# Attention with routed experts on one core: scores read three times from PSUM, q in zero-padded whole-array tiles, x gathered from the output

## The chip, the cores and the metric

One NeuronCore of one Trainium2 chip runs the whole program. The metric is device microseconds of one execution. The profile names the engines: PE is TensorE (PEld its weight loads), DVE VectorE, ACT ScalarE, POOL GpSimd, SP the SyncE queue that issues most DMAs. TensorE's clock is granted at one of two levels, 1.2 and 2.4 GHz; the profile prints the granted clock as a share of 2.4 GHz.

## The reference

```python
scores = matmul(q, k.T) / sqrt(64)            # 8 batches x 8 heads, 576 x 576, head size 64
scores = where(scores >= max(scores) - tau, scores, -1e9)
attn = exp(scores - max(scores)); attn /= attn.sum(-1) + 1e-9
x = (attn @ v) as (4608 tokens, 512)          # heads side by side
do_compute = x @ w_skip > 0                   # others: out = x
e = argmax(x @ w_gate)                        # one of 8 experts, weight gw from a softmax
out = x + gw * (relu(x @ w1[e]) @ w2[e])      # 512 -> 1024 -> 512
```

All inputs and the output are float32.

## The kernel before

The work has two parts. The attention part goes through 32 pairs of heads (8 batches, 4 pairs each). Of a pair's 576 query rows it takes four chunks of 128 rows, each for both heads, and a fifth chunk of the two heads' 64 last rows, one head above the other. A chunk has a unit per head, the fifth chunk one unit for both, so a pair has nine units, each with 128 rows by 576 scores. The expert part then runs nine jobs: one job for the fullest expert, picked early, and one per expert.

A unit before the change goes this way. `score` (line 516) makes the scores in two PSUM banks: the two heads lie in rows 0 to 63 and 64 to 127 of the array, and their matmuls run beside each other (the last chunk: `score_m`, line 525). `top` (line 540) is one custom DVE instruction that reads the two banks, scales by -1/8, writes the result `s` to SBUF and takes its minimum, which is minus the row's largest score. The banks are free when it is done; there are two slots of two banks (`NSL`), and a chunk takes both. `thr` (line 556) makes the threshold on POOL or DVE, `expo` (line 561) the exponential on ACT from `s`, `mask` (line 571) keeps p where `s` is under the threshold, on DVE, with both inputs in SBUF (four buffers `s`, `SB`; three chunks of p, `PFB`). Then `fph` (line 606) rounds p to float16 on ACT or DVE, `fpl` (line 621) subtracts for the low half on POOL or DVE, `turn` (line 627) issues two DMA transposes on SP, and `plan_av` (line 642) multiplies by v with 30 matmuls. `plan_out` (line 680) divides by the row sums, `plan_logits` (line 786) makes the routing logits, `plan_rows` (line 830) and `plan_tails` (line 843) store x twice: to `out`, where it stays for skipped tokens, and to a second DRAM copy `xs`, from which the expert jobs gather. `plan_v` (line 369) splits a batch's v into float16 halves.

The order on every engine is fixed when the program is built: `Plan.run` (line 132) is a list scheduler with a cost per operation and offsets (`OFF`, line 74) to the due times; an operation allowed on several engines goes to the one that can start first. Rings (`ring.take`, `ring.free`) make an operation wait until the buffer's last user is done. Where PE would idle by the plan, `fill` (line 1374) issues matmuls on zeros whose result nobody reads. POOL, SP and the other queues run in order.

In the expert part `gather_x` (line 1411) gathers a job's rows with indirect DMAs on POOL, `prep_x` (line 1419) transposes them on PE, `store` (line 1480) writes results to `out` with indirect DMAs on POOL. For most jobs the next job's gather is queued right behind a job's stores.

Of the kernel before, what the change touches and what calls it, by code (L numbers as in the profile page):

```python
# [12 lines left out]
F32 = mybir.dt.float32  # L13
# [11 lines left out]
P = 128  # L25
S = 576
# [26 lines left out]
GPB = 2  # L53
SB = 4
PFB = 3
NSL = 2
TOP = 3.0e38
FILL = (0.4, 0.22, 0.6)
# [16 lines left out]
    ld=-63.5, qs=-113.0, S=-99.4, mx=-53.9, th=-2.3, e=-9.8, p=-0.5, ph=-18.0, pl=11.4, tt=-64.0, av=31.6, cp=-20.0, x=28.2, xw=39.6, row=38.9, rsp=74.8, init=19.6, L1=-102.6, sc=-126.0, d0=16.6, phD=43.5, v=45.4, vsp=-12.1, V2=35.8,  # L75
# [20 lines left out]
class Plan:  # L96
    def __init__(self):
        self.ops, self.rings, self.fill = [], {}, None
# [33 lines left out]
    def run(self, look):  # L132
# [14 lines left out]
        while left:  # L147
# [13 lines left out]
            if e == "PE":  # L161
                if self.fill and free[e] > 0:
                    gap = t - free[e] - FILL[0]
                    for _ in range(int(gap * FILL[2] / FILL[1]) if gap > 0 else 0):
                        self.fill(half)
                half = o.half
# [20 lines left out]
def attn_moe_kernel(ctx: ExitStack, tc: tile.TileContext, qk, vl, vt, tau, wg, w1, w2, out):  # L187
# [14 lines left out]
    xs = dp.tile([NTOK, DM], F32, name="xs")  # L202
    taub = cp.tile([P, 1], F32, name="taub")
    nc.scalar.dma_start(taub, tau.rearrange("(a b) -> a b", b=1).broadcast_to([P, 1]))
    tneg8 = cp.tile([P, 1], F32, name="tneg8")
    nc.vector.tensor_scalar(tneg8, taub, 0.0, -0.125, op0=ALU.is_ge, op1=ALU.mult)
    wgt = cp.tile([P, NDT, 16], F32, name="wgt")
    onesr = cp.tile([1, P], F32, name="onesr")
    none16 = cp.tile([P, S], BF16, name="none16")
    nc.vector.memset(none16, 0.0)  # L210
# [6 lines left out]
    nc.vector.tensor_scalar(taue, taub, 0.0, None, op0=ALU.max)  # L217
    lstc = lst.rearrange("(p c) b -> p c b", p=P)
# [9 lines left out]
    ps_s = att.enter_context(tc.tile_pool(name="ps_s", bufs=1, space=PSUM))  # L228
    sall = ps_s.tile([P, 2 * NSL, 512], F32, name="sps")
    slots = [(2 * i, 2 * i + 1) for i in range(NSL)]  # L230
    rest = ps_s.tile([P, 512], F32, name="rest")
# [7 lines left out]
    PTa = ep.tile([P, PTB, 2 * STEP, P], F16, name="PTa", tag="QK1")  # L239
    hls = [hla[:, i] for i in range(HLB)]  # L240
# [5 lines left out]
    TMs = [a1.tile([P, STEP + 1, P], F16, name=f"TM{i}") for i in range(2)]  # L246
    def settle_v():
        nc.vector.memset(vraw[TL:P, NTL : NTL + H, :], 0.0)
        nc.vector.memset(vraw[0:TL, NTL + H :, :], 0.0)
# [77 lines left out]
    def gather(dst, idx, n):  # L327
# [3 lines left out]
            xs[0:n, :],  # L331
# [14 lines left out]
    def init():  # L346
# [6 lines left out]
            xs[NTOK - S - TL : NTOK - S, :].rearrange("p (o c) -> p o c", c=P),  # L353
# [3 lines left out]
    def plan_pair(g):  # L357
        k = STEP * g

        def load():  # L360
            T["raw", g] = wtile(F32, "raw")[:, 0 : 2 * S]
            nc.sync.dma_start(T["raw", g], qk[g])

        o = pl.dma(k - OFF["ld"], load, ring.take("wr", WRB) + T["start"], [2.2], 0.46)
        T["in", g] = o
# [3 lines left out]
    def plan_v(b):  # L369
# [90 lines left out]
        for i, (t0, t1) in enumerate(((0, NTL // 2), (NTL, NBK), (NTL // 2, NTL))):  # L460
# [19 lines left out]
            off = {DVE: OFF["d0"]} if b else {}  # L480
            r = pl.op(kk, fr, [sc], {ACT: w / 1200 + 0.15, DVE: w / 1900 + 0.1}, off=off)
            c = pl.op(kk + 0.1, fh, [r], {ACT: w / 1200 + 0.15, DVE: w / 1900 + 0.1}, off=off)
            d = pl.op(kk + 0.2, fl, [c], {POOL: 0.00208 * w + 0.075, DVE: w / 960 + 0.1}, off=off)
# [10 lines left out]

    def plan_chunk(g, i):
# [4 lines left out]
        hs = (slice(0, D), slice(D, P))  # L500

        if M:
            pr = slots.pop(0)
            slots.append(pr)
            views = [sorted(pr)]
        else:
            p1, p2 = slots.pop(0), slots.pop(0)
            views = [sorted((p1[u], p2[u])) for u in units]
            order = [views[u].index(p1[u]) for u in units]
            slots.extend(tuple(v) for v in views)  # L510
# [1275 lines left out]
```

## Time and profile before

| | us |
|---|---|
| median of 3 runs | 1115.29 (1114.37 to 1116.28) |
| the profiled execution | 1115.98 |
| its span, first to last instruction | 1114.1 |
| busy: PE, DVE | 874.4, 892.6 |
| busy: ACT, POOL | 525.1, 637.0 |
| mean granted clock | 0.826 |

The attention part lasts until about 800 us, the expert part from there to the end. A share of busy time over the whole span mixes the two. In the rows, `L545` is line 545, `p<-s,mx,p` names what is written and read, `x288` counts instructions, and what follows `<-` behind an idle time is what ended it. A float32 matmul counts as two instructions.

### The profile page before, as it was taken

What the parts mean: (1) busy time and instruction counts of PE and PEld (TensorE: products, weight loads), DVE (VectorE), ACT (ScalarE), POOL (GpSimd) and SP (SyncE); (2) the same over time, 40 slices, a digit from 0 to 9 for tenths busy, and PEclk for the clock granted to TensorE, in tenths of its full rate; (3) what the DMA queues carried; (4) which work ended last, traced back from release to release, by engine and by line L of the source; (5) the groups of instructions that cost most, each with busy time, mean ns of one, the idle gap of its engine ahead of it and who ended that gap; (6) DMA issues with size and microseconds to landing.
All of it is one profiled execution on the core that took longest, in us unless ns stands there. A gap on an engine that the chain in (4) does not pass through costs nothing. (4 is left out here: it accounts for less than half of the span.)

```text
span 1114.1 us, 21828 instructions
## 1 busy us (share of the span) xinstructions
PE 874.4 (78%) x8443; PEld 659.3 (59%) x8443; DVE 892.6 (80%) x1587; ACT 525.1 (47%) x785; POOL 637.0 (57%) x441
## 2 busy tenths in 40 slices
PE   7767777678878667887767877677679899999995
PEld 4445545446655445555444645454467699899994
DVE  6999998988898899999998999988944354557871
ACT  2745545553544455454445655555423243344441
POOL 1866655765775667536754675577631454544561
PEclk8787789777786887887688689687968999999998
DMA  5696896798659779977867879567871644445530
GB/s 168 132 204 131 139 250 133 139 195 204 129 121 233 146 145 186 225 148 138 173 163 146 163 153 240 118 113 179 152 236 56 228 150 161 161 160 185 191 132 16
DMA packets 387784, 179.34 MB, mean 161 GB/s; under 512 B 354231, under 2 KB 354999, under 8 KB 387680
## 3 DMA queue, kind: packets, MB, share of 16 engines
q1 hardware_dynamic: 383056, 167.78, 66.6%
q0 software_dynamic: 4480, 10.15, 2.7%
q8 instruction: 67, 1.10, 0.4%
q14 instruction: 37, 0.30, 0.1%
q10 hardware_dynamic: 144, 0.00, 0.0%
HBM read 67.76 MB, written 24.65 MB: 83 GB/s over the span
## 5 line engine op out<-in xcount | busy, mean ns | idle before, releaser
L521 PE MATMUL sps<-raw 64*128 64x288 f32 x1024 | 227.0, 558 | 155.8 <-DVE mx L545 154.1
L623 POOL TENSOR_TENSOR hla<-p,hla 128x1152 f16<-128x1152 f32 x102 | 263.5, 2586 | 56.9 <-ACT hla L339 27.1
L574 DVE SCALAR_TENSOR_TENSOR p<-s,mx,p 128x576 f32<-128x576 f32 x256 | 280.5, 1120 | 4.5 <-POOL mx L559 2.3
L545 DVE CUSTOM_DVE_ANT_0 s<-sps,none,tneg 128x576 f32<-128x576 f32 x288 | 225.7, 810 | 54.6 <-PE sps L521 52.4
L567 ACT ACTIVATE p<-s,mx 128x576 f32<-128x576 f32 x256 | 187.7, 768 | 152.6 <-DVE mx L545 105.8
L521 PEld LDWEIGHTS sps<-raw 64*128 64x128 f32 x1024 | 109.7, 239 | 212.7 <-DVE mx L545 189.0
L664 PEld LDWEIGHTS <-PTa 128*128 128x128 f16 x3840 | 157.4, 110 | 56.6 <-issue 51.1
L664 PE MATMUL avp<-Vh,PTa 128*128 128x65 f16 x2560 | 170.9, 211 | 1.1 <-ACT a L339 0.6
L559 POOL TENSOR_SCALAR mx<-mx,taue 128x2 f32<-128x2 f32 (+1 forms) x88 | 71.9, 818 | 158.9 <-DVE mx L545 145.1
L664 PE MATMUL avp<-Vl,PTa 128*128 128x64 f16 x1280 | 160.9, 210 | 1.5 <-DVE Vl L474 1.5
L339 ACT ACTIVATE hla<-p 128x1152 f16<-128x1152 f32 x113 | 130.1, 1155 | 49.3 <-DVE p L574 49.3
L1407 POOL TENSOR_TENSOR wl<-wr,wh 128x1024 fp32r<-128x1024 f32 x28 | 72.3, 2597 | 29.5 <-ACT wh L1406 24.1
L1376 PE MATMUL rest<-none 64*128 64x512 bf16 (+1 forms) x233 | 86.0, 463 | 0.0
L531 PE MATMUL sps<-raw 64*64 64x288 f32 (+2 forms) x320 | 51.5, 463 | 36.8 <-DVE mx L545 36.3
L1444 PE MATMUL hps<-xh,wh 128*128 128x288 f32 (+4 forms) x224 | 69.1, 308 | 0.1
L714 POOL TENSOR_TENSOR xb<-a,z 128x512 f32<-128x512 f32 x32 | 46.7, 1458 | 38.5 <-DVE z L705 30.2
L1444 PE MATMUL hps<-xl,wh 128*128 128x288 f32 (+4 forms) x224 | 67.9, 303 | 0.0
L1444 PE MATMUL hps<-xh,wl 128*128 128x288 f32 (+4 forms) x224 | 67.8, 303 | 0.0
L531 PEld LDWEIGHTS sps<-raw 64*64 64x64 f32 x320 | 30.0, 168 | 62.9 <-DVE mx L545 43.4
L1484 POOL DMA_INDIRECT out<-o,ids x20 | 20.2, 1008 | 74.6 <-DVE o L1483 26.9
L623 POOL TENSOR_TENSOR hm<-pm,hm 128x576 f16<-128x576 f32 x29 | 42.6, 1470 | 32.5 <-ACT hm L339 28.0
L339 ACT ACTIVATE a<-avp 128x260 f32<-128x260 f32 (+1 forms) x96 | 31.3, 344 | 63.4 <-PE avp L664 62.7
(244 smaller groups left out, 1606.9 us busy)
## 6 DMA issues: line engine op xcount, KB each, us to landing
wr<-in_w SPq DMA_DIRECT2D x31, 1024.0 KB, 5.5
raw<-in_qk SPq DMA_DIRECT2D x32, 576.0 KB, 4.9
vraw<-in_vl SPq DMA_DIRECT2D x32, 256.0 KB, 4.1
xs<-xb SPq DMA_DIRECT2D x32, 256.0 KB, 3.9
out<-xb SPq DMA_DIRECT2D x32, 256.0 KB, 3.2
PTa<-hla SPq DMA_TRANSPOSE x256, 3.1
vraw<-in_vt SPq DMA_DIRECT2D x8, 128.0 KB, 3.9
TM<-hm SPq DMA_TRANSPOSE x64, 3.0
```

Source lines behind the costliest of these rows:

```text
L339: nc.scalar.activation(dst, src, AF.Copy)
L521: nc.tensor.matmul(bank(h, j)[:, 0:HS], x[hs[h], i * P : i * P + P], x[hs[h], k0 : k0 + HS], start=True, stop=True)
L531: nc.tensor.matmul(bank(0, j)[hs[h], o : o + w], x[hs[h], NM * P : S], x[hs[h], S + c0 : S + c0 + w], start=True, stop=True, skip_group_ch ...
L545: nc.vector.tensor_tensor_reduce(T["s", g, i, u].rearrange("p (a b) -> p a b", a=2), bank(u), none16[:, 0:S].rearrange("p (a b) -> p a b", ...
L559: (nc.gpsimd if e == POOL else nc.vector).tensor_scalar(m[:, 1, cs], m[:, 0, cs], taue, None, op0=ALU.add)
L567: nc.scalar.activation(T["p", g, i][:, u], T["s", g, i, u], AF.Exp, bias=T["mx", g][:, 0, c : c + 1], scale=-1.0)
L574: nc.vector.scalar_tensor_tensor(p, T.pop(("s", g, i, u)), T["mx", g][:, 1, c : c + 1], p, op0=ALU.is_le, op1=ALU.mult)
L623: (nc.gpsimd if e == POOL else nc.vector).tensor_tensor(hl[:, lo0 : lo0 + w], T.pop(("p", g, i)).rearrange("p a b -> p (a b)"), hl[:, 0:w] ...
L664: nc.tensor.matmul(o[:, 0:e], x[:, w_, cs], y[:, vb, 0:e], start=first and j == 0, stop=kt == NM and j == 2, skip_group_check=True,)
L1376: nc.tensor.matmul(rest, none16[0:r, 0:P], none16[0:r, 0:512], start=True, stop=True, skip_group_check=True)
L1407: lo[q % 2].tensor_tensor(w[1][:, sl], rs, w[0][:, sl].bitcast(F32), op=ALU.subtract)
L1444: nc.tensor.matmul(hp_[:, 0:cap], w_, x, start=(i == 0), stop=(i == len(mm) - 1))
```

## The change

Scores. k is loaded alone (`kt`, three buffers) and scaled by 1/8 on ACT (the first on DVE). q is loaded by two DMAs of 64 partitions each into one of two float32 tiles of 128 x 1152 whose other halves are zero, set once on POOL: head 0's q in rows 0 to 63 and columns 0 to 575, head 1's in rows 64 to 127 and columns 576 to 1151, its last 64 queries first. Each unit's scores are then matmuls of the whole array (128 rows, two of 288 columns; for head 1 the first is split in two), and the last chunk takes the 128 columns in the middle. A unit has a PSUM tile of two banks for itself, from a ring of three (`SPB`), and the tile is free only after `mask`. The ring of small PSUM tiles `gps` shrinks from two to one.

Softmax. `top` is a plain maximum on DVE, `thr` goes to ACT, `expo` reads PSUM and writes `e` (three buffers), `mask` reads PSUM and `e` and writes p (two chunks). `fph` is on ACT alone, `fpl` on POOL alone; v's splitting too is on ACT and POOL alone, but for the first batch. `fill` is gone.

x. It is stored once, to `out`; gathers read `out`. No declaration is added that a gather doesn't depend on the stores into `out`.

```diff
-    OFF: ld=-63.5, qs=-113.0, S=-99.4, mx=-53.9, th=-2.3, e=-9.8, p=-0.5, ph=-18.0, pl=11.4, tt=-64.0, ...
+    OFF: ld=1.2, qs=-97.2, S=24.7, mx=-53.4, th=-79.8, e=-1.0, p=-17.9, ph=-22.6, pl=-42.8, tt=40.9, ...
...
+        def loadq():
+            q = QZs[g % QB]
+            for h in range(2):
+                nc.sync.dma_start(q[h * D : h * D + D, h * S : h * S + S], qq[g][h * D : h * D + D])
...
+                        ps[:, j, o : o + w], q[:, at : at + P], k[:, c0 : c0 + w], start=True, stop=True,
...
-            nc.vector.tensor_tensor_reduce(
-                T["s", g, i, u].rearrange("p (a b) -> p a b", a=2),
-                bank(u),
...
+            nc.vector.tensor_reduce(
+                T["mx", g][:, 0, c : c + 1], bank(u), AX.XY, ALU.max, negate=True
+            )
...
+            nc.scalar.activation(m[:, 1, cs], m[:, 0, cs], AF.Identity, bias=ntau, scale=-1.0)
...
+            nc.scalar.activation(e, bank(u), AF.Exp, bias=T["mx", g][:, 0, c : c + 1])
...
             nc.vector.scalar_tensor_tensor(
-                p, T.pop(("s", g, i, u)), T["mx", g][:, 1, c : c + 1], p, op0=ALU.is_le, op1=ALU.mult
-            )
+                T["p", g, i][:, u].rearrange("p (a b) -> p a b", a=2),
+                bank(u),
+                T["mx", g][:, 1, c : c + 1],
+                T.pop(("e", g, i, u)),
+                op0=ALU.is_ge,
+                op1=ALU.mult,
+            )
...
+            k = pl.op(n + OFF["p"] + 0.1 * u, lambda u=u: mask(u), [t, es[u]] + take, {DVE: 0.73})
+            ring.free("sps", [k])
+            ring.free("e", [k])
...
-            xs[0:n, :],
+            out[0:n, :],
...
-            for i, dst in enumerate((xs, out)):
```

## Rows read from the trace of the kernel before

**Rows 1.** The page's busy times, and of its 40 slices the DVE row, in tenths.
```profile
PE 874.4 (78%) x8443; PEld 659.3 (59%) x8443; DVE 892.6 (80%) x1587; ACT 525.1 (47%) x785; POOL 637.0 (57%) x441
DVE  6999998988898899999998999988944354557871
```

**Rows 2.** Busy time in stretches of the attention part: the stretch, its us, busy us (instructions) of PE, PEld, DVE, ACT and POOL, granted clock, busy share of the 16 DMA engines, GB/s.
```profile
100.00:200.00 100.00, 72.31 (x861) 49.85 (x860) 93.77 (x162) 51.78 (x76) 58.91 (x36) 0.85 0.87 174
200.00:300.00 100.00, 77.89 (x851) 55.09 (x851) 89.18 (x166) 49.82 (x74) 67.00 (x43) 0.74 0.78 165
300.00:400.00 100.00, 74.43 (x849) 51.98 (x849) 91.13 (x157) 51.41 (x75) 62.88 (x40) 0.78 0.80 164
400.00:500.00 100.00, 77.36 (x917) 53.64 (x916) 92.61 (x170) 52.70 (x78) 57.41 (x37) 0.78 0.88 179
500.00:600.00 100.00, 72.15 (x737) 47.80 (x738) 89.54 (x147) 45.63 (x67) 60.92 (x42) 0.74 0.73 154
600.00:700.00 100.00, 77.31 (x917) 54.99 (x913) 95.95 (x185) 58.27 (x84) 63.35 (x41) 0.82 0.88 184
```

**Rows 3.** Single lines of the code: engine, count, shortest, median and longest duration in ns, first and last start in us.
```profile
L545 DVE CUSTOM_DVE_ANT_0 s<-sps,none,tneg x288: 750/810/819, 13.9 to 793.8; 128x576 f32<-128x576 f32 x144
L574 DVE SCALAR_TENSOR_TENSOR p<-s,mx,p x256: 759/815/3781, 15.8 to 795.3; 128x576 f32<-128x576 f32 x128
L623 POOL TENSOR_TENSOR hla<-p,hla x102: 2357/2388/3368, 21.6 to 800.9; 128x1152 f16<-128x1152 f32 x102
```

**Rows 4.** The order of time in two places: start us, us, engine, instruction, and in brackets the idle time before it.
```profile
399.69 0.80 DVE L545 CUSTOM_DVE_ANT_0 s<-sps,none,tneg 128x576 f32<-128x576 f32 x1
399.75 2.38 POOL L623 TENSOR_TENSOR hla<-p,hla 128x1152 f16<-128x1152 f32 x1
...
412.35 2.37 POOL L623 TENSOR_TENSOR hla<-p,hla 128x1152 f16<-128x1152 f32 x1 [2.82 <-ACT hla L339]
...
413.20 2.87 DVE L574 SCALAR_TENSOR_TENSOR p<-s,mx,p 128x576 f32<-128x576 f32 x2
...
417.47 1.55 DVE L574 SCALAR_TENSOR_TENSOR p<-s,mx,p 128x576 f32<-128x576 f32 x2
```

**Rows 5.** Groups of instructions: busy us, mean ns of one, idle time before them and what ended it. All but the last are of the stretch to 820 us with shapes kept apart; the last is the page's, the fill matmuls.
```profile
L574 DVE SCALAR_TENSOR_TENSOR p<-s,mx,p 128x576 f32<-128x576 f32 x256 | 280.5, 1120 | 4.5 <-POOL mx L559 2.3 <-ACT p L567 1.6
L545 DVE CUSTOM_DVE_ANT_0 s<-sps,none,tneg 128x576 f32<-128x576 f32 x288 | 225.7, 810 | 54.6 <-PE sps L521 52.4 <-PE sps L531 1.7
L567 ACT ACTIVATE p<-s,mx 128x576 f32<-128x576 f32 x256 | 187.7, 768 | 152.6 <-DVE mx L545 105.8 <-POOL hla L623 26.2 <-DVE hla L623 9.2
L339 ACT ACTIVATE hla<-p 128x1152 f16<-128x1152 f32 x113 | 130.1, 1155 | 49.3 <-DVE p L574 49.3
L559 POOL TENSOR_SCALAR mx<-mx,taue 128x2 f32<-128x2 f32 x71 | 58.8, 828 | 130.5 <-DVE mx L545 120.9 <-DVE vmx L436 5.4 <-DVE vmx L415 4.0
L559 DVE TENSOR_SCALAR mx<-mx,taue 128x2 f32<-128x2 f32 x57 | 40.4, 710 | 0.3
L623 DVE TENSOR_TENSOR hla<-p,hla 128x1152 f16<-128x1152 f32 x26 | 37.5, 1442 | 0.1
L409 DVE TENSOR_REDUCE vmx<-vraw 128x1 f32<-128x1280 f32 x16 | 23.0, 1474 | 3.1 <-DMA vraw<-in_vl 3.1
L1376 PE MATMUL rest<-none 64*128 64x512 bf16 (+1 forms) x233 | 86.0, 463 | 0.0
```

**Rows 6.** In the order of time, at the higher clock (first three rows) and at the lower (last two): one chunk's 30 weight loads for the product with v, half a chunk's scores (two matmuls beside each other, 4 instructions), one chunk's scores (8 instructions); then one chunk's scores and one chunk's weight loads.
```profile
153.28 0.97 PEld L664 LDWEIGHTS <-PTa 128*128 128x128 f16 x30 [0.42 <-issue]
...
156.37 0.76 PE L521 MATMUL sps<-raw 64*128 64x288 f32 x4
...
161.08 1.24 PE L521 MATMUL sps<-raw 64*128 64x288 f32 x8 [2.09 <-DVE mx L545]
...
413.33 2.29 PE L521 MATMUL sps<-raw 64*128 64x288 f32 x8 [7.23 <-DVE mx L545]
...
415.55 1.66 PEld L664 LDWEIGHTS <-PTa 128*128 128x128 f16 x30 [0.76 <-issue]
```

**Rows 7.** The stretches around them, columns as in Rows 2.
```profile
150.00:160.00 10.00, 8.05 (x123) 6.15 (x123) 9.98 (x14) 5.37 (x8) 3.99 (x3) 1.00 1.08 280
410.00:420.00 10.00, 6.45 (x74) 4.67 (x75) 9.74 (x16) 6.81 (x9) 7.22 (x5) 0.58 0.48 105
```

**Rows 8.** DMA issues: what is written and read, queue, count, KB each, median us from issue to landing. `in_vt` goes to 64 partitions, `in_vl` to 128.
```profile
raw<-in_qk SPq DMA_DIRECT2D x32, 576.0 KB, 4.9
vraw<-in_vl SPq DMA_DIRECT2D x32, 256.0 KB, 4.1
...
vraw<-in_vt SPq DMA_DIRECT2D x8, 128.0 KB, 3.9
...
out<-o,ids POOLq DMA_INDIRECT x20, 2.8
```

**Rows 9.** POOL in the expert part, in the order of time: one of seven places where the next job's gathers follow a job's last store.
```profile
1035.47 0.99 POOL L1484 DMA_INDIRECT out<-o,ids  x1 [0.17 <-issue]
1036.76 2.30 POOL L328 DMA_INDIRECT xg<-xs,idg  x1 [0.30 <-DVE ej L1619]
```

**Rows 10.** Waits of TensorE in the expert part from 860 us on, all over 1 us in sum: us in total, times, longest.
```profile
PE xtp L1426 <- DMA xg<-xs,idg: 3.2, 2, 2.0
PE yps L1525 <- POOL wl L1407: 1.9, 2, 1.2
```

More of the change, by code (lines that the diff above doesn't have):

```diff
@@ L52 @@
 SPB = 3
[L53 to L58, printed above, removed]
+GPB = 1
+EB = 3
+PFB = 2
+QB = 2
+KB = 3
 HLB = 3
@@ L161, in run @@
             if e == "PE":
[L162 to L165, printed above, removed]
                 half = o.half
@@ L186, in attn_moe_kernel @@
 @with_exitstack
-def attn_moe_kernel(ctx: ExitStack, tc: tile.TileContext, qk, vl, vt, tau, wg, w1, w2, out):
+def attn_moe_kernel(ctx: ExitStack, tc: tile.TileContext, qq, kk_, vl, vt, tau, wg, w1, w2, out):
     nc = tc.nc
@@ L227, in attn_moe_kernel @@
     a1 = att.enter_context(tc.tile_pool(name="a1", bufs=1))
[L228 to L231, printed above, removed]
+    ps_s = att.enter_context(tc.tile_pool(name="ps_s", bufs=SPB, space=PSUM))
     ps_t = att.enter_context(tc.tile_pool(name="ps_t", bufs=GPB, space=PSUM))
@@ L239, in attn_moe_kernel @@
     PTa = ep.tile([P, PTB, 2 * STEP, P], F16, name="PTa", tag="QK1")
+    QZs = [a1.tile([P, 2 * S], F32, name=f"QZ{i}") for i in range(QB)]
     hls = [hla[:, i] for i in range(HLB)]
@@ L358, in plan_pair, with loadk, scale @@
         k = STEP * g
[L360 to L365, printed above, removed]
+        def loadk():
+            T["k", g] = ap_.tile([P, S], F32, name="kt", tag="kt", bufs=KB)
+            nc.sync.dma_start(T["k", g], kk_[g])
+        def loadq():
+            q = QZs[g % QB]
+            for h in range(2):
+                nc.sync.dma_start(q[h * D : h * D + D, h * S : h * S + S], qq[g][h * D : h * D + D])
+        def scale(e):
+            x = T["k", g]
+            if e == ACT:
+                nc.scalar.activation(x, x, AF.Copy, scale=tpos)
+            else:
+                nc.vector.tensor_scalar(x, x, tpos, None, op0=ALU.mult)
+        o = pl.dma(k - OFF["ld"], loadk, ring.take("kt", KB) + T["start"], [1.15], 0.46)
+        x = pl.op(k - OFF["qs"], scale, [o], {ACT: 0.57} if g else {DVE: 0.42})
+        y = pl.dma(k - OFF["ld"] + 0.1, loadq, [(o,)] + ring.take("qz", QB) + T["zero"], [0.75, 0.75])
+        T["in", g] = [x, y]
         if g == 0:
@@ L493, in defer, with sps @@
         later.append((u + DU, f))
+    def sps():
+        return ps_s.tile([P, 2, 512], F32, name="sps", tag="sps")
     def plan_chunk(g, i):
@@ L614, in fph @@
             w = len(units) * S
-            copy(e, T["hl", g, i][:, 0:w], T["p", g, i].rearrange("p a b -> p (a b)"))
+            copy(ACT, T["hl", g, i][:, 0:w], T["p", g, i].rearrange("p a b -> p (a b)"))
         w = len(units) * S
@@ L1340, in attn_moe_kernel @@
     T["start"], T["settle"] = [], []
+    T["zero"] = [pl.op(-150, blank_q, [], {POOL: 1.0})]
     plan_pair(0)
@@ L1372, in attn_moe_kernel @@
     ms.enter_context(tc.manual_schedule(engines={ET.PE, ET.DVE, ET.Activation, ET.Pool, ET.SP}))
-    def fill(half):
-        r = D if half else P
-        nc.tensor.matmul(rest, none16[0:r, 0:P], none16[0:r, 0:512], start=True, stop=True, skip_group_check=True)
-    pl.fill = fill
     pl.run(LOOK)
```

174 lines of the change are left out of this document (66 added, 108 removed).

## The prediction, made before the changed kernel was built or run

> **What bounds the kernel now.** I read the page's busy times first, then the stretches of the attention part, then the lines that fill the busiest engine, and the order of time where a mean and a median of one line disagree. Over the whole span PE and DVE look alike, but the slices show DVE at nine tenths until the 28th and at half after it [rows 1]: two parts with two bounds. From 100 to 700 us DVE is busy 552.2 of 600 us, 92%; POOL 370, 62%; ACT 310, 52%; the DMA engines 0.82 on the mean; the granted clock 0.785 on the mean [rows 2]. So DVE bounds the attention part. The 32 pairs take from 13.9 to 793.8 us [rows 3], that is 24.4 us a pair, or 2.71 us for each of its nine units. I work in these, against the profiled execution's 1115.98 us; the median of the runs lies 0.7 us under it, which changes nothing below.
>
> The mask's mean is 1.12 us, though its median is 0.815 and its longest 3.78 [rows 3, 5]. The order of time shows why: two masks issued at 413.20 while POOL subtracts until 414.72 end at 416.07, as if they had begun when POOL was done; two others take 1.55 [rows 4]. The custom instruction never passes 0.82, and took 0.80 beside the same POOL work [rows 3, 4]. It reads one operand from PSUM, the mask both from SBUF.
>
> **The change part by part.**
>
> DVE. After it, 288 masks have one operand in PSUM. The trace has no such mask; bounds are 0.74 (what the second of two undisturbed masks adds, 1.55 less 0.815) and the present 1.12. I take 0.78, half of 1.55, since the instruction with one PSUM operand is not held up: 288 x (1.12 - 0.78) = 98 us less. The Trainium skill (SBUF — State Buffer, "Who interferes with whom") says that a DVE instruction with at most one SBUF input does not contend with GpSimd, while one with two waits for a whole GpSimd instruction that reads SBUF. The trace's 0.80 beside POOL agrees; no run so far shows the new mask.
>
> The maximum replaces the custom instruction: a plain reduction of 1280 elements takes 1.474 us, so 576 cost 0.66 by size; the upper bound is the custom one's 0.81 [rows 5]. I take 0.74, between them: 288 x 0.07 = 20 us less. The thresholds and subtractions leave DVE (40.4 + 37.5 us) [rows 5]. Sum 98 + 20 + 40 + 37 = 195 us, 6.1 a pair. DVE falls from 0.92 x 24.4 = 22.4 to 16.3 us a pair, 15.2 to 19.8 by the bounds. Smaller moves (some rounding, most of v's splitting) would take it lower and are not counted.
>
> ACT. It now has 0.52 x 24.4 = 12.6 us a pair. It gets 15 roundings of two units more (128 - 113, at 1.155 us, 17 us), 160 thresholds, 31 scalings of k (0.77 by the exponential's row, 24 us) and v's pieces. The trace has no threshold on ACT; below lies nothing, above the 0.77 of an instruction over 288 times the columns; I take 0.2, near the low end, because two columns are next to none: 32 us. With v's pieces, some 20 pieces of 1 us, that makes 93 us, 2.9 a pair: 15.5. The exponential from PSUM I leave at 0.77, bounds plus and minus 0.1.
>
> POOL loses its thresholds (71 of 0.83 us = 59) and gets 26 subtractions of 2.39 (62) and v's. 15.1 a pair stays about 15 to 16.
>
> PE. Two matmuls beside each other take 0.76 us at the higher clock and a chunk's two such pairs 1.24, so a matmul is 0.48 and the tail of the last 0.28; at the lower clock a chunk takes 2.29, a matmul about twice 0.48 [rows 6, 7]. Afterwards a unit needs two in a row, 0.96 or 1.9; nine are 8.6 or 17.3 us a pair. The products with v, five of 0.97 or 1.66 [rows 6], add 4.9 or 8.3: 13.5 or 25.6. With the clock as now (0.785 is 43% of the time at the lower level) a pair takes 1 / (0.57/13.5 + 0.43/25.6) = 17, with about 2 for logits 19. The fills' 86 us go [rows 5]. PE, which halved its scores by taking two heads beside each other, is then near a bound.
>
> DMA. 0.82 x 24.4 = 20.1 us a pair of all engines. A pair loses one 256 KB store into the second copy; at the 280 GB/s of a saturated stretch [rows 7] that is 0.94 us. The bytes of q and k stay. I take 19.2 as for q loads that cost by their bytes; the other bound is below, as a rival. On SP a pair issues two loads more and one store fewer, ahead of transposes in the same order; I cost the one issue more at nothing as long as the transposes wait for roundings. The single tile for logits makes their transposes, copies and products follow each other; they stand behind x and nothing waits for them but the next pair's, so nothing again, and if PE has to wait in its order, at most the 2 us a pair that they are worth.
>
> PSUM. A tile was free after the first DVE instruction; now it is held from its scores to its mask. Undisturbed: 0.96 for scores, 0.96 for the other head's (the threshold needs both maxima), 0.74 maximum, 0.77 exponential, 0.78 mask, and some 0.6 that I estimate for four hand-overs: 4.8 us. Three tiles then give one unit in 1.6 us, 14.4 a pair: no bound. In a queue, one product with v on PE (0.97), one rounding on ACT (1.155) and two masks on DVE (1.56) can stand ahead: 8.5 us, 25.5 a pair. Half of these gives 6.65 us, 20 a pair.
>
> So five resources want 15 to 19 us of what was 24.4, and DMA (19.2) and PE (19) want most. DVE was filled to 0.92 behind four buffers and three chunks of p; with three PSUM tiles and two chunks it will be less. If nothing gained in filling, 0.79 would give 24.4 again. I take the middle, 0.86: 19.2 / 0.86 = 22.3 us a pair, and (24.4 - 22.3) x 32 = 67 us less.
>
> Expert part. A gather reads what stores write, so it waits until a store has landed, 2.8 us from issue, where it now starts 1.3 after it [rows 8, 9]: 1.5 us later, seven times; behind it on POOL stand the subtractions of the weights, on which PE waits too. PE already waits twice for a gather and twice for those [rows 10]. If only these four pass it on, 6 us; bounds 0 and 7 x 1.5 = 10.5. Between the parts the fills before the first expert layer go; their cover was the higher clock there. I set 3 us for a few us at half speed, bounds 0 and 7. Two stores fewer on SP in front of the first gather give back 1 to 2.
>
> Sum: 1116 - 67 + 6 + 3 - 2 = 1056 us.
>
> **The rivals.**
>
> PSUM is the bound, and it gets slower. Place: the score matmul of unit n+3 waits for the mask of unit n. It decides where the holding time passes 3 x 2.71 = 8.1 us. At 8.5 us a pair takes 25.5: 1116 + 35 + 7 = 1158; with the scores at the lower clock (+2 us for two) 9.5 us and 1254 would be the far end. For it: today PE waits for the very same kind of release, DVE's, and those releases come late because of queues. Against it: DVE's queue gets shorter by a third.
>
> The queues hardly matter: DMA or PE is filled to 0.92 as DVE was. 19.2 / 0.92 = 20.9 us a pair: 1116 - 112 + 7 = 1011.
>
> q costs two whole loads of DMA time. A load of 128 KB into 64 partitions lands after 3.9 us, one of 256 KB into 128 after 4.1 [rows 8]: half the bytes, nearly the time. If each half of q costs as 256 KB, 0.94 us, 2 x 0.94 stand in place of half of the present 576 KB (1.05), 0.83 a pair more: 20.0 / 0.86 = 23.3, and 1116 - 35 + 7 = 1088. The Trainium skill (SBUF — State Buffer, "Can I just issue two DMAs to hit both halves?") says that loads into two halves of the partitions serialize; the landing times above don't contradict it, and no row shows the two halves' rate.
>
> The clock falls. Without fills, and with PE waiting for PSUM, 70% of the time at the lower level gives 1 / (0.3/13.5 + 0.7/25.6) + 2 = 22.2 on PE, at 0.92 24.2: 1116 - 6 + 7 = 1117, about no change. Against it: PE has more work and less idle time. That the change doesn't do what it says, masks staying at 1.12 beside POOL, would put DVE at 19.4, level with DMA: 0.86 of that gives 22.5 and 1062, inside the forecast's own range.
>
> **How the numbers follow.** Forecast 0.38; DMA by halves 0.14; full queues 0.13; PSUM slower 0.30; the clock 0.05. A difference of 0.2%, 2.2 us, is about what can be told from no change. Faster are the first three, less 0.03 that falls near zero; with 0.04 for no change and the rest slower: 0.62, 0.04, 0.34. The range goes from 985 (below the full queues' 1011, for the lower bounds of the mask and the handing over) to 1175, which takes in the PSUM case at 8.5 us and leaves out its far end. The forecast's own range is 1030 to 1085.
>
> **What would show it.** Right: the mask's mean near its median; DVE at 65 to 75% from 100 to 600 us; a pair in 22 to 23 us; PE busier with the clock not lower. The PSUM case: the score matmuls' idle time ends on the mask and grows, while DVE's idle time before the maximum, now 54.6 us [rows 5], grows with it and no engine passes 80%. The DMA case: a share over 0.9 with products waiting for transposes. In the expert part: gathers that wait for `out`, and more than two waits of PE for them. The prediction is wrong if a pair takes over 24.4 us, or if masks keep lasting over 1 us.

## The result, and the profile after

The changed kernel takes 1010.56 us (median of 4 runs, 1007.83 to 1013.37) against 1115.78 us before (4 runs beside it): a ratio of 0.9058, with a 95% interval of 0.9031 to 0.9085. The prediction said 1056 us and a range of 985 to 1175: the sign and the range hold, the size was too small by 45 us. Ratios leave out executions that ran slower than the others of the same kernel for no reason of its own; this matters for one kernel below (the first layer on the score tiles), where two of four are left out and the ratio isn't that of the medians.

Where the time went is read from three marks of the two profiled executions (1115.98 and 1010.29 us): the first and the last row maximum on DVE, and the first matmul of the early job's first layer.

| us | before | after | difference |
|---|---|---|---|
| start to first maximum | 13.9 | 12.2 | -1.7 |
| first to last maximum (attention) | 779.9 | 653.1 | -126.8 |
| last maximum to layer 1 of the early job | 48.2 | 39.7 | -8.5 |
| from there to the end of the span | 272.1 | 303.5 | +31.4 |
| span | 1114.1 | 1008.5 | -105.6 |

So a pair of heads takes 20.4 us instead of 24.4, and a quarter of that gain is given back behind the first matmul of the early job. The page after the change, where [rows 1] stood: busy times of PE and DVE, and DVE, granted clock and DMA share in 40 slices.

```profile
PE 837.2 (83%) x8274; PEld 719.3 (71%) x8274; DVE 674.4 (67%) x1143; ACT 609.9 (60%) x1020; POOL 593.4 (59%) x398
...
DVE  6888878788787787876767878982134565526431
...
PEclk9999999989999997998999899975998999988998
DMA  6999999999999999899999899993046543453420
```

The nines have moved from DVE's row to that of the DMA engines, and they end at the 27th slice. The stretches of the attention part, columns as in [rows 2]:

```profile
100.00:200.00 100.00, 87.90 (x1110) 74.62 (x1107) 76.83 (x120) 83.88 (x142) 73.86 (x42) 0.98 1.07 195
200.00:300.00 100.00, 81.42 (x942) 68.95 (x940) 81.21 (x138) 71.07 (x120) 68.97 (x45) 0.95 1.04 193
300.00:400.00 100.00, 83.34 (x993) 70.43 (x994) 75.01 (x124) 74.70 (x126) 65.23 (x38) 0.94 1.04 197
400.00:500.00 100.00, 87.18 (x1010) 73.18 (x1009) 77.71 (x126) 75.22 (x126) 71.46 (x44) 0.92 0.95 174
500.00:600.00 100.00, 82.96 (x991) 69.50 (x990) 78.60 (x132) 72.55 (x122) 66.00 (x41) 0.93 0.97 185
```

DVE is busy 78% (92% before), PE 85%, ACT 75%, POOL 69%, the DMA share is 1.01 (it can pass 1, as in [rows 7], so 1 isn't its ceiling), and the granted clock 0.944 on the mean where it was 0.785: PE is at the higher of its two levels most of the time. What TensorE waited for from 100 to 600 us (us, times, longest), the two longest:

```profile
PE sps L522 <- DVE p L554: 39.0, 30, 3.9
PE avp L643 <- DMA PTa<-hla: 20.7, 18, 3.0
```

The first is a wait for masks, which free the score tiles, the second for transposes of p. The groups that answer to [rows 5], shapes kept apart, of the stretch to 830 us (L534 is the maximum, L546 the exponential, L541 the threshold, L603 the subtraction on POOL):

```profile
L534 DVE TENSOR_REDUCE mx<-sps 128x1 f32<-128x576 f32 x288 | 215.3, 752 | 113.3 <-PE sps L522 111.8
L554 DVE SCALAR_TENSOR_TENSOR p<-sps,mx,e 128x576 f32<-128x576 f32 x256 | 197.8, 807 | 13.9 <-POOL hla L603 5.3 <-ACT e L546 5.0 <-ACT mx L541 2.8
L546 ACT ACTIVATE e<-sps,mx 128x576 f32<-128x576 f32 x288 | 205.5, 730 | 29.6 <-DVE mx L534 25.6 <-DVE vki L439 1.7
L541 ACT ACTIVATE mx<-mx,ntau 128x2 f32<-128x2 f32 x128 | 37.6, 294 | 71.2 <-DVE mx L534 70.6 <-DVE vki L443 0.4
L603 POOL TENSOR_TENSOR hla<-p,hla 128x1152 f16<-128x1152 f32 x128 | 305.1, 2385 | 162.2 <-ACT hla L336 112.4 <-DMA PTa<-hla 20.0 <-issue 8.7
```

The mask (L554) has a mean of 0.807 us where it had 1.120. The order of time shows it, as in [rows 4]: two masks beside a subtraction on POOL.

```profile
411.47 2.39 POOL L603 TENSOR_TENSOR hla<-p,hla 128x1152 f16<-128x1152 f32 x1
...
411.81 1.53 DVE L554 SCALAR_TENSOR_TENSOR p<-sps,mx,e 128x576 f32<-128x576 f32 x2
```

They end at 413.34, while POOL works until 413.86. In [rows 4] the like pair took 2.87 us and ended only after POOL. This is what the Trainium skill states (SBUF — State Buffer, "Who interferes with whom"): with at most one SBUF input, and outside its 2-port modes, a DVE instruction doesn't contend with GpSimd. The trace agrees: all 256 masks of the four full chunks lie between 0.795 and 0.820 us.

In the expert part two things are new. PE in the early job's first layer, start us, us, idle before in brackets:

```profile
709.66 0.56 PE L1204 MATMUL gps<-QK,wh 128*128 128x320 f32 x2 [1.05 <-DVE QK L1210]
...
712.74 0.56 PE L1204 MATMUL gps<-QK,wh 128*128 128x320 f32 x2 [1.05 <-DVE QK L1210]
```

Each of its eight blocks waits until ACT and DVE have emptied the one small PSUM tile; the layer takes 24.8 us (705.0 to 729.8), before 14.0 (842.0 to 856.0). And POOL, where a job's gathers follow a job's last store, to be held against [rows 9]:

```profile
917.51 0.99 POOL L1452 DMA_INDIRECT out<-o,ids  x1 [0.17 <-issue]
923.89 1.27 POOL L325 DMA_INDIRECT xg<-out,idg  x1 [5.40 <-DMA out<-o,ids]
```

The gather starts 6.4 us after the store, before 1.3. TensorE's waits from 660 us on, which answer to [rows 10] (us, times, longest):

```profile
PE yps L1493 <- POOL wl L1375: 11.7, 2, 6.4
PE gps L1204 <- DVE QK L1210: 7.4, 7, 1.1
PE xtp L1394 <- DMA xg<-out,idg: 5.6, 3, 4.2
...
PE yps L1474 <- POOL wl L1375: 4.2, 1, 4.2
```

Gathers (xtp) and the weights' subtractions behind them on POOL (wl) now cost PE 21.5 us, where [rows 10] has 5.1.

### The profile page after: what moved, and what is told of

The parts are those of the page before. It is cut to its first block, busy times and chain, and to the rows that moved or that the text cites. A ratio compares the mean times of both kernels' runs of the same rounds, so it can differ in the third digit from the quotient of the medians.

```text
span 1008.5 us, 21609 instructions
## 1 busy us (share of the span) xinstructions
PE 837.2 (83%) x8274; PEld 719.3 (71%) x8274; DVE 674.4 (67%) x1143; ACT 609.9 (60%) x1020; POOL 593.4 (59%) x398
## 3 DMA queue, kind: packets, MB, share of 16 engines
q8 instruction: 66, 1.08, 0.4%
## 5 line engine op out<-in xcount | busy, mean ns | idle before, releaser
L522 PE MATMUL sps<-kt,QZ 128*128 128x288 f32 (+2 forms) x1408 | 353.1, 400 | 70.3 <-DVE p L554 58.8
L603 POOL TENSOR_TENSOR hla<-p,hla 128x1152 f16<-128x1152 f32 x128 | 305.1, 2385 | 162.2 <-ACT hla L336 112.4
L522 PEld LDWEIGHTS sps<-kt,QZ 128*128 128x128 f32 x1408 | 248.9, 201 | 120.6 <-issue 57.4
L534 DVE TENSOR_REDUCE mx<-sps 128x1 f32<-128x576 f32 x288 | 215.3, 752 | 113.3 <-PE sps L522 111.8
L546 ACT ACTIVATE e<-sps,mx 128x576 f32<-128x576 f32 x288 | 205.5, 730 | 29.6 <-DVE mx L534 25.6
L554 DVE SCALAR_TENSOR_TENSOR p<-sps,mx,e 128x576 f32<-128x576 f32 x256 | 197.8, 807 | 13.9 <-POOL hla L603 5.3
L643 PEld LDWEIGHTS <-PTa 128*128 128x128 f16 x3840 | 140.6, 101 | 52.0 <-DMA PTa<-hla 28.9
L336 ACT ACTIVATE hla<-p 128x1152 f16<-128x1152 f32 x128 | 148.5, 1161 | 32.0 <-DVE p L554 15.5
L541 ACT ACTIVATE mx<-mx,ntau 128x2 f32<-128x2 f32 (+1 forms) x160 | 47.0, 294 | 78.8 <-DVE mx L534 77.1
L1374 ACT ACTIVATE wh<-wr 128x1024 fp32r<-128x1024 f32 x60 | 60.6, 1050 | 0.0
L1474 PE MATMUL yps<-wh,QK 128*128 128x512 f32 (+2 forms) x224 | 57.1, 405 | 1.7 <-ACT wh L1374 1.5
L1375 DVE TENSOR_TENSOR wl<-wr,wh 128x1024 fp32r<-128x1024 f32 x32 | 46.0, 1445 | 9.6 <-ACT wh L1374 9.3
```

What stands on the lines that cost most here:

```text
L336: nc.scalar.activation(dst, src, AF.Copy)
L522: nc.tensor.matmul(ps[:, j, o : o + w], q[:, at : at + P], k[:, c0 : c0 + w], start=True, stop=True, skip_group_check=True,)
L534: nc.vector.tensor_reduce(T["mx", g][:, 0, c : c + 1], bank(u), AX.XY, ALU.max, negate=True)
L541: nc.scalar.activation(m[:, 1, cs], m[:, 0, cs], AF.Identity, bias=ntau, scale=-1.0)
L546: nc.scalar.activation(e, bank(u), AF.Exp, bias=T["mx", g][:, 0, c : c + 1])
L554: nc.vector.scalar_tensor_tensor(T["p", g, i][:, u].rearrange("p (a b) -> p a b", a=2), bank(u), T["mx", g][:, 1, c : c + 1], T.pop(("e", ...
```

## The experiments

Twelve kernels, in four groups. "Attention" is the time from the first to the last maximum of the run's profile; ratios are to the kernel before.

**The mask's operands and how long PSUM is held.** The first kernel is the one before with a mask that reads its scores from PSUM, the slots held until then; its two slots of two banks stay.

```diff
-                p, T.pop(("s", g, i, u)), T["mx", g][:, 1, c : c + 1], p, op0=ALU.is_le, op1=ALU.mult
+                p, bank(u), T["mx", g][:, 1, c : c + 1], p, op0=ALU.is_ge, op1=ALU.mult
...
-            ring.free("sps", [m])
...
             ring.free("s", [k])
+            ring.free("sps", [k])
```

> The kernel before with one part of the change: the mask reads its scores from PSUM (threshold times -8) and the two slots of two banks stay taken until the mask. The exponential, the half-array scores, POOL's and DVE's shares and the second copy of x stay. Theory (masks no longer wait for POOL, DVE was the bound): the mask's mean falls from 1.12 to 0.80 us, some 95 us of DVE time go, but with only two slots, both taken by one chunk, scores must wait for masks and eat part of it; time 1040 to 1110. Rival (holding PSUM until the mask costs more than the port): the mask falls as well, and the time rises over 1116, DVE idle before the maximum rising from 55 us to over 150. Rival (lighter DMA or the clock made the gain): the time stays within 1105 to 1125 although DVE has 95 us less to do.

Measured: 1241.72 us, ratio 1.114 (1.1095 to 1.1184), attention 925.3 us, 28.9 a pair. Two of its groups, to 830 us:

```profile
L521 PE MATMUL sps<-raw 64*128 64x288 f32 x904 | 196.8, 556 | 159.8 <-DVE p L575 129.2 <-DVE pm L575 28.7 <-DVE vki L428 1.9
...
L575 DVE SCALAR_TENSOR_TENSOR p<-sps,mx,p 128x576 f32<-128x576 f32 x224 | 173.3, 812 | 13.9 <-ACT p L567 5.4 <-POOL mx L559 0.3 <-ACT vraw L466 0.2
```

The mask loses its wait for POOL (0.812 us), and the kernel gets 128 us slower all the same, since the score matmuls now wait for masks: the rival was right in its time, the theory's gain didn't come. DVE's idle time before the maximum rose to 98 us, not to the rival's 150; it was ACT, before the exponential, that waited most for DVE's maximum (287 us, before 106). Half of the change, without the room that it needs, is a loss. The second kernel goes the other way: the changed kernel, with a mask that compares the exponential with exp(-tau) and so has both operands in SBUF.

```diff
-                bank(u),
-                T["mx", g][:, 1, c : c + 1],
-                T.pop(("e", g, i, u)),
+                e,
+                ethr,
+                e,
```

> The changed kernel, but the mask takes the exponential twice from SBUF and compares it with exp(-tau), so that it has two SBUF operands again; all else and the order of work stay (a PSUM tile may be free one step earlier, which could only help). Theory (two SBUF operands make a mask wait for POOL): the mask's mean rises from 0.81 to 1.1 to 1.4 us, longest over 2.5; DVE gets 80 to 170 us more, 78% busy becomes over 90%, and the attention part gets 30 to 110 us longer: 1040 to 1120. Rival (DMA bounds it whatever DVE does): the mask's mean rises too, but the time stays under 1025. Rival (the mask was short for another reason): its mean stays at 0.81.

Measured: 1107.31 us, ratio 0.9947 (0.9924 to 0.9970), attention 746.8 us (+93.7). Its masks, and two of them in the order of time:

```profile
L557 DVE SCALAR_TENSOR_TENSOR p<-e,ethr 128x576 f32<-128x576 f32 x256 | 368.2, 1466 | 24.2 <-ACT e L548 15.0 <-POOL hla L606 4.2 <-ACT hla L338 3.0
...
411.98 4.68 DVE L557 SCALAR_TENSOR_TENSOR p<-e,ethr 128x576 f32<-128x576 f32 x2
413.16 2.88 POOL L606 TENSOR_TENSOR hla<-p,hla 128x1152 f16<-128x1152 f32 x1
```

Two masks take 4.68 us beside one subtraction; their mean over all is 1.466 us, and DVE is busy 93% from 100 to 600 us. The theory holds: with the rest of the change in place, that one operand lies in PSUM is worth most of the gain. The third takes one PSUM tile from the changed kernel.

```diff
-SPB = 3
+SPB = 2
```

> The changed kernel with two PSUM tiles for scores instead of three. A unit now takes 2.27 us (20.4 a pair), so with three tiles a tile may be held 6.8 us on the mean, and the prediction's undisturbed hold is 4.8 us. Theory (the hold has slack only because of the third tile): two tiles need hold / 2 a unit, 2.4 us at 4.8 and 3.3 us at the 6.65 that the prediction took, 21.6 to 30 a pair; attention 690 to 960 us, the time 1050 to 1310, the score matmuls' idle time behind the mask above 150 us where it is now 59. Rival (the DMA engines set the pace and PSUM is far from it): attention 650 to 680 us, the time 1005 to 1035.

Measured: 1141.95 us, ratio 1.0239 (1.0212 to 1.0266), attention 787.3 us, 24.6 a pair.

```profile
L522 PE MATMUL sps<-kt,QZ 128*128 128x288 f32 x896 | 300.0, 455 | 112.7 <-DVE p L554 111.6 <-DVE vmx L420 0.8
```

The time and the pair lie in the theory's range; the score matmuls' idle time behind masks was put too high (116 us over all shapes, 61 after the change). A unit takes 2.73 us, so a tile was held at most 5.5 us on the mean. Held no longer than that, three tiles would allow 16.4 us a pair, so their number alone doesn't set 20.4, though TensorE still waits for masks with three.

**The second copy, the fills and the DMA engines.** The kernel before without its second copy, gathers from `out`:

```diff
-            for i, dst in enumerate((xs, out)):
+            for i, dst in enumerate((out,)):
...
-            xs[0:n, :],
+            out[0:n, :],
```

> The kernel before without the second copy of x: stored once, gathered from the output. Theory (DVE bound the attention part): attention unchanged within 8 us, first to last maximum 772 to 785; expert part 0 to 8 us longer by gathers that wait for stores; time 1108 to 1124. Rival (lighter DMA made the gain): 1 us a pair, 32 us less in the attention part; time 1080 to 1092.

Measured: 1160.15 us, ratio 1.0425 (1.0381 to 1.0469): slower, which no theory had. By the marks: attention 808.5 us (+28.6), from there to layer 1 40.5 (-7.7), from layer 1 to the end 293.6 (+21.5). With the first, the masks' mean goes from 1.120 to 1.177 us and ACT's wait for POOL before the exponential from 26.2 to 55.9 us. We take it for a by-product, since with fewer operations the list scheduler can put the others in another order; no run tests this. The last is the gathers' wait: the three kinds of waits above cost PE 21.2 us here. The changed kernel with the copy put back (the same lines the other way round):

> The changed kernel with the second copy of x put back and gathered from. Theory (DMA bounds the attention part at a share of 1.0, and gathers that wait for stores cost the expert part): attention gets 0.9 to 1.1 us a pair longer, 28 to 35 us, first to last maximum 653 becomes 681 to 690; TensorE's waits from the second expert layer on, 21 us for gathers and for weights split on POOL, fall to 6: 1010 becomes 1018 to 1032. Rival (DMA is hidden): attention unchanged within 6 us and the time falls to 992 to 1000.

Measured: 1002.32 us, ratio 0.8991 (0.8951 to 0.9032), 8 us less than without the copy (the intervals of the two ratios just meet), where the theory had it rise: attention 663.4 (+10.3), then 44.9 (+5.2), then 284.1 (-19.4). In the attention part the copy costs about a third of what was expected, with the reservation on the order of work just made, and the gathers' wait is again some 20 us. PE's waits of 100 to 600 us only trade places: 33.1 us for transposes and 25.2 for masks, where the changed kernel has 20.7 and 39.0. The kernel before without fills (`pl.fill = fill` left out):

> The kernel before without its fill matmuls on zeros. Theory (after the change the clock is high because PE has more work of its own): here, with nothing in their place, the clock from 100 to 700 us falls from 0.785 to 0.6 to 0.75, PE still hides behind DVE for the most part, and the time rises by 0 to 25 us. Rival (the fills themselves cost time by standing in PE's queue): the time falls by 5 to 20 us.

Measured: 1111.95 us (10 runs), ratio 0.9986 (0.9965 to 1.0007); the granted clock from 100 to 700 us is 0.783 on the mean, with fills 0.785. Neither the theory's fall of the clock nor the rival's gain came: in this stretch the fills held up nothing and raised no clock. Outside it they did. From 780 to 800 us the clock is 0.99 with fills and 0.71 without, and the early job's first layer takes 14.0 us with fills (clock 1.00) and 16.0 without (0.86); the time stays the same, since the layer starts 1.9 us sooner after the last maximum. The changed kernel with q loaded a second time, into a tile that nobody reads:

```diff
+            for h in range(2):
+                nc.sync.dma_start(QD[h * D : h * D + D, :], qq[g][h * D : h * D + D])
```

> The changed kernel with q loaded twice, the second time into a tile that nobody reads (two loads of 144 KB into 64 partitions each a pair). It prices these loads where DMA is the bound. By their bytes at 280 GB/s: 1.05 us a pair, 34 us in all, 1044. If each half costs as 256 KB into 128 partitions: 1.9 us a pair, 60 us, 1070. If DMA isn't the bound: under 1018.

Measured: 1048.95 us (1039.56 to 1053.38), ratio 0.9435 (0.9387 to 0.9482), attention 682.4 (+29.3): 0.92 us a pair for 288 KB in two halves of the partitions. The profiled execution was the fastest of the four; by the medians the loads cost 38 us, 1.2 a pair. What the packets of SP's queue took says it more directly (packets, MB, share of the span):

```profile
q1 hardware_dynamic: 388048, 167.79, 77.1%
```

That is 800 us of all engines (77.1% of 1037.8), 34 more than the 766 of the changed kernel: 1.05 us a pair, the price by bytes. The second copy, as many bytes into DRAM, took 38 (80.1% of 1004.7, less 766). The changed kernel without the DMA transposes of p's low half (the product takes the high half's block twice, so part of the result is left out):

```diff
         def turn(j):
+            if j:
+                return
```

> The changed kernel without the DMA transposes of the low halves: half of all transposes are not issued, and the product with v takes the high half in their place, so the result leaves out the low part of p. The order of work stays. Theory (DMA bounds the attention part): its share falls from 1.0 to about 0.65 and a pair from 20.4 us to the next bound, DVE, ACT or PE at 16 to 17 us of work each: 18 to 19 us a pair, the time 925 to 970. Rival (the PSUM tiles bound it, held until the mask): a pair stays at 20 us or more, time over 1000.

Measured: 983.43 us, ratio 0.8837 (0.8801 to 0.8874), attention 625.8 us, 19.6 a pair. Two of its stretches, columns as before:

```profile
200.00:300.00 100.00, 83.50 (x971) 70.40 (x970) 80.07 (x137) 72.91 (x123) 71.48 (x45) 0.93 0.54 116
300.00:400.00 100.00, 87.12 (x1089) 74.16 (x1088) 85.29 (x144) 80.33 (x137) 70.55 (x42) 0.98 0.65 132
```

The DMA share falls from 1.01 to 0.63, and a pair gets only 0.85 us shorter, less than the theory had. If the DMA engines are the bound, then by a narrow margin; PE, DVE and ACT stand close together at 80 to 86%. PE's waits for transposes are gone (none of them is left in its list from 100 to 600 us), and those for masks grow from 39.0 to 45.5 us. What sets 19.6 stays open.

**The whole array.** The changed kernel with the zero half of q left out of the score matmuls of the four full chunks, in the same order and with the same columns:

```diff
+            rs = slice(0, P) if M else slice(u * D, u * D + D)
...
-                        ps[:, j, o : o + w], q[:, at : at + P], k[:, c0 : c0 + w], start=True, stop=True,
+                        ps[:, j, o : o + w], q[rs, at : at + P], k[rs, c0 : c0 + w], start=True, stop=True,
```

> The changed kernel with the scores of the four chunks of 128 rows taken from the 64 rows of q and k that hold the head, the zero half left out of the matmul (the same results; the last chunk stays as it is). Theory (a matmul costs by its columns, and neither the zeros nor the whole array changes clock or price): attention 645 to 665 us, the granted clock from 100 to 600 us within 0.03 of 0.945, the time 1003 to 1022. Rival (work on the whole array is what raised the clock from the 0.785 of before): the clock falls to about 0.8, PE at 0.85 of 20.4 = 17.3 us a pair becomes 19 to 20.5, and the time goes to 1040 to 1100. Third case (two heads' matmuls in different halves run beside each other and PE gets shorter): PE's busy share falls by 5 points or more, but the DMA share of 1.0 keeps the time within 10 us.

Measured: 1054.70 us, ratio 0.9462 (0.9424 to 0.9499), attention 690.4 us (+37.3). Its stretches:

```profile
100.00:200.00 100.00, 88.96 (x1062) 70.86 (x1061) 74.81 (x117) 83.61 (x140) 73.00 (x41) 0.87 1.02 188
200.00:300.00 100.00, 88.00 (x851) 68.75 (x851) 67.56 (x120) 62.60 (x106) 61.00 (x41) 0.75 0.90 167
300.00:400.00 100.00, 88.99 (x972) 70.95 (x971) 70.74 (x110) 74.44 (x125) 66.14 (x39) 0.83 1.05 202
400.00:500.00 100.00, 84.27 (x916) 66.90 (x915) 74.61 (x130) 68.47 (x116) 66.61 (x44) 0.80 0.91 164
500.00:600.00 100.00, 88.96 (x958) 71.55 (x959) 71.87 (x119) 71.18 (x119) 63.58 (x37) 0.78 1.02 188
```

The clock falls to 0.806, PE is busier (88%) and does less, and a pair takes 21.6 us: the rival holds, with its clock and its time. At one and the same clock the price is the same: in a stretch at 1.00, the six instructions of one of head 1's units take 1.35 us on 64 rows (at 162.58 us) as on 128 in the changed kernel (at 154.31 us).

**The expert part.** The early job's transposes and first layer on the ring of three score tiles, free by then:

```diff
-            return g_tile().rearrange("p a b -> p (a b)")
+            return sps()[:, 0]
...
-            ring.free("gps", xo[-1:])
+            ring.free("sps", xo[-1:])
```

> The changed kernel with the early job's transposes and first layer on the ring of three score tiles (free by then) instead of the one small tile. That layer now takes 24 us from its first to its last matmul, before the change 13.5, and each of its blocks waits about 1 us for DVE. Theory (the ring of one makes matmul, ACT and DVE follow each other): the layer takes 12 to 15 us and the time falls by 8 to 12, to 998 to 1003. Rival (what comes behind it is late anyway, by the sorting or by weights from DMA): the layer gets shorter and the time stays within 3 us of 1010.

Measured: 999.78 us (987.66 to 1005.65), ratio 0.8886 (0.8835 to 0.8937), which makes some 992 us. With four executions 18 us apart it can't be told whether the time is the theory's 998 to 1003 or lower; the rival's, within 3 us of 1010, it isn't. The profiled execution took 1003.31. In it the layer takes 16.5 us (700.2 to 716.7), a little more than it said, and no longer waits for DVE; it begins 8.4 us sooner after the last maximum, at 31.3. But from its first matmul to the end it is 301.3 us, hardly less than 303.5, though the layer got 8.3 us shorter: 2.3 us of that go into longer waits for gathers, the rest isn't placed. With the gathers' waits out of the way as well:

```diff
+            ga = gather(j.xg[0:m, t, :], j.idg[0:m, t : t + 1], NTOK)
+            for x in rows:
+                tc.declare_no_dep(ga.ins, x.ins, reason="every token goes to one expert")
+            gets.append(ga)
...
-        for x in rows:
+        for x in rows + gets:
             tc.declare_no_dep(sc.ins, x.ins, reason="every token goes to one expert")
```

> The run before, and besides it declared that gathers of the expert part and the stores of results don't depend on each other (an expert's job gathers only its own tokens). Theory (a gather behind a job's stores waits for their landing, 5 to 6 us, and the weights' subtractions and PE behind it): gathers start 1 to 2 us after the last store, PE's waits for gathered rows and POOL's weight halves fall from 21.5 us to under 8, and the time falls by another 10 to 18, to 982 to 992. Rival (the wait only moves to weights that are late from DMA or to DVE): within 4 us of the run before, 996 to 1003.

Measured: 973.47 us (973.14 to 976.01), ratio 0.8719 (0.8700 to 0.8738), the fastest of all and under the theory's range. TensorE's waits from 660 us on:

```profile
PE xtp L1398 <- DMA xg<-out,idg: 3.9, 4, 1.3
...
PE yps L1497 <- POOL wl L1376: 1.9, 2, 1.2
```

From 21.5 us (23.8 in the run before) they fall to 5.8, and the stretch from layer 1 to the end is 274.5 us, where before the change it was 272.1. So without the gathers' wait the layer's gain arrives too, as the next run shows. The declaration alone:

> The changed kernel with only the declaration that gathers of the expert part and the stores of results don't depend on each other; the first layer stays on the one small tile. With both edits the time was 973.5, with the score tiles alone 999.8 on the mean of runs that spread from 988 to 1006, so the declaration's own share is between 15 and 32 us. Theory (the gathers' wait is a loss of its own, 27 us by the two profiles, 301.3 less 274.5 from the first matmul of layer 1 to the end): that stretch falls from 303.5 to 276 to 280 and the time to 981 to 987, while the first layer stays at 24 us. Rival (a good part came only because the shorter first layer lets the later jobs start sooner): the stretch stays over 287 and the time at 992 to 1000.

Measured: 989.49 us (989.08 to 992.75), ratio 0.8888 (0.8860 to 0.8916). The layer still takes 24.6 us (708.9 to 733.5), the stretch falls to 282.0, and the time ends 2.5 us above the theory's range: the theory holds, a little smaller, and the rival doesn't. POOL at the same place as above:

```profile
912.55 0.99 POOL L1456 DMA_INDIRECT out<-o,ids  x1 [0.17 <-issue]
913.84 2.31 POOL L325 DMA_INDIRECT xg<-out,idg  x1 [0.30 <-DVE ej L1591]
```

The gather starts 1.3 us after the store, as in [rows 9]. Of the 31.4 us that the expert part lost, 21.5 are the gathers' wait (303.5 to 282.0), 7.5 the small tile (282.0 to 274.5), and 2.4 are left. The 21.5 have two parts. PE's waits for gathers and weights fall by 16.8 us (21.5 to 4.7). And behind the first layer PE's own instructions take 238.1 us at a granted clock of 0.97, where the changed kernel needs 242.5 us at 0.94 for as many: 4.4 us that the waits cost besides their own length.

## Why the prediction was right in sign and short in size

**The step that failed: "I take the middle, 0.86".** The needs of the engines were sized well. A pair's busy time after the change, share times 20.4 us, beside the forecast: DVE 15.9 (16.3), ACT 15.4 (15.5), POOL 14.1 (15 to 16), PE 17.3 (19), DMA 20.7 (19.2). What was wrong is how full the fullest of them would be. The argument was that with three PSUM tiles and two chunks of p no engine reaches the 0.92 of DVE before. By the forecast's own 19.2 us, DMA is filled to 0.94 of 20.4, and by its measured share to 1.01. That is the rival "the queues hardly matter" with 20.9 us and 1011. That its price was right to 0.5 us a pair is luck: a DMA time 1.5 us too low and a filling of 0.92 in place of 1.01 cancel.

That DMA sets the pair isn't shown by its share. With the copy back the share was 1.06 and a pair only 0.32 us longer, without half the transposes it was 0.63 and a pair 0.85 us shorter, and in the changed kernel PE waits longer for masks (39.0 us) than for transposes (20.7). A slower PE (half the array, 1.2 us a pair), slower masks (2.9) and a tile less (4.2) each lengthen the pair. So several resources stand close to what a pair takes, and which sets 20.4 stays open.

**DMA time.** The step "a pair loses one 256 KB store", 0.94 us less, is right in bytes and wrong in time. The page's rows of SP's queue, packets, MB, and the packets' time as a share of the span, before and then after:

```profile
q1 hardware_dynamic: 383056, 167.78, 66.6%
```

```profile
q1 hardware_dynamic: 382928, 158.35, 76.0%
```

Fewer bytes take more time: 742 us of all engines before (66.6% of 1114.1), 766 after, and the transposes' median from issue to landing goes from 3.1 to 3.8 us. These are not the same transfers, but the run with two tiles, which issues those of the changed kernel at a slower pace, is:

```profile
q1 hardware_dynamic: 382928, 158.35, 65.2%
```

Its packets took 741 us (65.2% of 1135.8). So with transfers denser in time each one's packets last longer, and the share isn't a fixed need that can be divided by a filling; with the copy back the same engines moved 201 GB/s on the mean of 100 to 600 us, without it 189.

**The masks and DVE.** 0.807 us instead of the 0.78 taken, inside its bounds; the maximum 0.752 instead of 0.74; DVE's 6.1 us a pair less was 6.5. Right, and the run with both operands in SBUF shows the reason: it gives back 93.7 of 126.8 us. What the sum left out is the custom instruction's second part, which reads out its accumulator and went with it, 0.7 us a pair:

```profile
L545 DVE DVE_READ_ACCUMULATOR2_ANT mx<- 128x1 f32 x288 | 23.0, 80 | 0.0
```

(The upper bound of 19.8 us a pair is 20.0 by its own terms, which changes nothing.)

**ACT.** The threshold took 0.294 us, not 0.2, 15 us more in all; the exponential 0.730, not 0.77, some 11 us the other way.

**PE and the clock.** "With the clock as now" was the second error. At 0.944 the prediction's own formula gives 16.2 us a pair instead of 19, and 17.3 is measured. The rival "the clock falls" had the sign wrong: in the attention part fills gave no clock, and the scores on the whole array raise it. The run with half the array puts this at 37 us of attention (44 us of the time, by the medians). The prediction counted the doubled score time as PE's loss and didn't ask what the whole array does to the clock.

**PSUM.** The holding time was taken as 6.65 us; two tiles show at most 5.5, near the undisturbed 4.8. The rival's mechanism exists: it decides with two tiles (24.6 us a pair, and 28.9 in the kernel before with its slots by chunk), while with three it is one wait among others. Of the signs named for it, one came all the same: DVE's idle time before the maximum went from 54.6 to 113.3 us. But the score matmuls' idle time behind DVE fell, from 190 us to 61, and PE is busy 85%.

**q by halves.** 288 KB cost 1.05 us a pair of the engines' time and 0.92 (profile) to 1.2 (medians) of the pair, where bytes at the saturated rate give 1.05 and "two whole loads" 1.88: that rival falls. The Trainium skill (SBUF — State Buffer, "Can I just issue two DMAs to hit both halves?") says that two such loads serialize. Whether they do can't be seen here; beside other traffic they took no more of the engines' time than their bytes.

**The expert part.** "If only these four pass it on, 6 us" is the term that was mis-sized: 21.5. Two things were wrong in it. Of POOL's waits before gathers, 0.3 us before, three became 5.4 to 5.6 us and the other four 2.4 to 2.6 (26 us over seven places), so they are 2.1 to 5.2 us later and not 1.5; why three wait longer isn't shown. And PE passes on most of it, and loses clock by it. "So nothing again" for the single small tile looked only at the logits; in the early job's transposes and first layer it costs 16 us, 989.49 less 973.47 (the layer starts 8.2 us later behind the last maximum, and the stretch from it is 7.5 longer). That two stores fewer "give back 1 to 2" was too little: without the copy the stretch between the parts is 7.7 us shorter in the one pair of kernels and 5.2 in the other. The lower clock without the fills was about right: the first block's matmul pairs take 0.73 us (granted clock 0.50) where later ones take 0.46 (1.00), some 2 us in all, as in the kernel before without fills (16.0 us for the layer, not 14.0), against 3 set.

So the sum 1116 - 67 + 6 + 3 - 2 was in truth 1116 - 127 + 21: attention 60 us better, the rest 14 us worse.

## What to carry to other kernels

Give a two-input DVE instruction that runs beside GpSimd work one operand in PSUM, and buy the PSUM tiles for the longer hold in the same edit. The operand without the room lost 128 us here, and 26 us with two tiles; the room without the operand left the time about where it was (0.9947). When a second DRAM copy goes, look at what the reads of the one left now wait for: where indices can't meet, declaring that was worth 21 us, twice what putting the copy back cost in the attention part. When a ring shrinks, go through all its users, also those in parts far from the change.

## What the runs showed of the hardware that was not expected

Scores on half of the array's rows ran at a granted clock of 0.806 with PE 88% busy; the same scores on all rows, half of them zeros, at 0.944 with PE 85% busy. Multiplying by zeros took 37 us off the attention part. The fills of the kernel before, matmuls on zeros put where PE would idle, changed nothing from 100 to 700 us (0.785 with them, 0.783 without), and raised the clock only outside it, as from 780 to 800 us (0.99 with them, 0.71 without).

The DMA share isn't a load that fills up at 1. The same transfers took 741 us of the engines with two score tiles and 766 with three, at a faster pace. With the copy back the share reached 1.08, and the engines still took more: 256 KB more a pair cost 0.32 us, while 288 KB of q cost 0.92 to 1.2.

A wait of TensorE can cost more than its length: without the gathers' waits, 16.8 us of them, PE's own instructions behind the first layer took 4.4 us less as well, at a granted clock of 0.97 instead of 0.94.
